# w_out2 in Strassen's form for the first super-block too, and the factors made at 1.4 pieces a step

## The chip, the cores and the metric

One core of a Trainium2 chip runs the whole kernel. The metric is the device time of one execution, in microseconds (us). The engines named below are PE (TensorE, the matmuls), PEld (its weight loads), ACT (ScalarE), DVE (VectorE), POOL (GpSimd) and SP (SyncE, which issues most DMAs).

## What is computed

Three layers follow one another on 2304 tokens of width 512, all in float32.

```python
# retention: 4 batches, 8 heads, 576 positions, 64 wide; Dmat[i, j] = gamma**(i - j) for i >= j
ret = (q @ k.T) * scale * Dmat
x = (ret @ v)                                   # 2304 x 512
h = x @ w_in                                    # 512 -> 2048
g = where(h >= 1, h, where(h <= -1, 0, (h + 1)**2 / 4))
x = g @ w_out                                   # 2048 -> 512
out = ((x @ w_a) * (x @ w_b)) @ w_out2          # 512 -> 1536 -> 512
```

The change concerns the last line alone. Float32 precision is reached by splitting each operand into a rounded upper part and the rest, so that one product takes three matmuls (upper by upper, rest by upper, upper by rest; `HL`, line 479).

## The kernel before

Work is written as a program over tiles of 128 partitions. A planner puts it into one queue per engine when the program is built (`schedule_with_timeline_sim`, line 1380): an instruction that was written earlier goes first, but one that waits for data or for a free buffer is passed by later ones. So plain matmuls of one piece of work stand in the gaps of another. The first part, down to line 1193, is ordered by hand.

Stage 0 is the retention with the first w_in pieces. Stages 1 and 2 (the loop at line 1211) take the other pieces of w_in and w_out, one `step` for each pair of a piece and a block of 384 or 512 tokens: `l1` makes 12 matmuls, `act1` the activation on ACT and DVE, `l2` of the step before 12 more. Beside them runs `maker` (line 325), a generator that turns w_a and w_b, and in `last_tiles` (line 359) w_out2, into the seven left factors of Strassen's product, in Winograd's form. Each `yield` ends a piece of it. It converts two raw 64-bit tiles into `stage` (one buffer; ACT lines 200 and 201, DVE lines 207, 210, 217), takes four sums and differences, splits every factor into its two parts (ACT cast, DVE subtraction) and stores them to DRAM (`q`, `o`). There are 60 pieces for w_a and w_b and 30 for w_out2, one pair of w_out2 tiles in five. `make_more` (line 397) makes one piece when two weight tiles are free; in stages 1 and 2 it is called as often as `credit` allows, which grows by PACE x width / 384 a step (line 1229).

Weights live in a pool of 17 tiles of 512 KB, and one more. `take` and `used` count them. `load_to` (line 413) fetches finished factors on SP's queue in the order of `loads`; it keeps `least` tiles free.

The third layer handles the tokens in three super-blocks of 768 (the loop at line 1285). Each has twelve `Quad`s, one for each of w_a and w_b and six pairs of w_out2's rows; a quad is seven products of six matmuls, into the accumulators named qx, qy and qz, and two quads meet in an elementwise product. In super-blocks 1 and 2 this product goes by `act2_blocks` into four blocks per three pairs, and `second_layer` (line 978) multiplies them with w_out2's factors: seven products over three pieces r, 12 matmuls each (`l2_product`). The right operands come from `cut` (line 927): ACT casts a block into a buffer of the pool `sp`, DVE subtracts the rest; `next_half` orders a cut one turn ahead of its product. `minus` makes the differences of blocks, `keep` (line 832) evacuates an accumulator on ACT.

In super-block 0 it is otherwise. `act2` multiplies 384 columns at a time, `split_g` splits, and `l2_2` (line 1030) multiplies with plain w_out2 tiles, which `last_tiles` keeps as `weights[f]`: the first half of the tokens into the accumulators `acc` between the quads (`fill`), the other half afterwards into `late`. So plain w_out2 tiles occupy weight tiles until their last use, and the pool `y` holds results until then.

Of the kernel before, what the change touches and what calls it, by code (L numbers as in the profile page):

```python
# [20 lines left out]
P = 128  # L21
# [13 lines left out]
NF2 = 12  # L35
HT = 384
WBUFS, WBUFS2 = 17, 1
PACE = 1.2
MID = 288
CHUNKS = 4  # L40
YBUFS = 5
# [83 lines left out]
def retention_ffn_kernel(  # L125
# [233 lines left out]
    def last_tiles(f0, f1):  # L359


        o11, o21, o12, o22 = range(4)
        for p in range(f0 // 2, f1 // 2):
            r, i = divmod(p, 2)
            st = stage.tile([P, 8, 256], F32, tag="stage", name="stage")
            for j in range(2):
                f = 2 * p + j
                t = convert(raws2.next(), st[:, 2 * j:2 * j + 2, :].rearrange("p c f -> p (c f)"))
                weights[f] = split(t, take(f))
                raws2.more()  # L370
                yield
            for j, f, m in ((0, 2 * p, 0), (2, 2 * p + 1, 0), (6, 2 * p + 1, 1)):
                nc.sync.dma_start(
                    od[j][r][:, i, :].rearrange("p (a c) -> p a c", a=2),
                    weights[f][:, :, 256 * m:256 * m + 256].bitcast(F32),
                )
            sub, add = nc.vector.tensor_sub, nc.vector.tensor_add
            add(st[:, S1], st[:, o21], st[:, o22])
            sub(st[:, S2], st[:, S1], st[:, o11])
            sub(st[:, S3], st[:, o11], st[:, o21])  # L380
            sub(st[:, S4], st[:, o12], st[:, S2])
            yield
            for k, pair in enumerate((((1, S1), (3, S2)), ((4, S4), (5, S3)))):
                t = take(("mo", p, k)).tile([P, 2, 512], F32R, tag="w", name="qo")
                for n, (j, o) in enumerate(pair):
                    hi, lo = t[:, n, :256], t[:, n, 256:]
                    nc.scalar.copy(hi, st[:, o])
                    nc.vector.tensor_sub(lo, st[:, o], hi.bitcast(F32))
                    nc.sync.dma_start(od[j][r][:, i, :], t[:, n, :].bitcast(F32))
                used(("mo", p, k))  # L390
                yield
            if i == 1:
                banked.update(("o", j, r) for j in range(7))

# [11 lines left out]
    loads = []  # L406
    for n in range(B * S // (2 * HT)):
        loads += [(n, p, k) for p in range(NF2 // 2) for k in range(7)]
        if n:
            loads += [(n, "o", j, r) for j in TURNS for r in range(NF2 // 4)]  # L410
    begun2, held_back = [0], [0]

    def load_to(n):
        while begun2[0] < min(n, len(loads)):
            key = loads[begun2[0]]
            least = 3 if raws2.taken < len(second) else 1 + held_back[0]
            if key[1:] not in banked or free() < least:
                return
            t = weights[key] = take(key).tile([P, 2, 512], F32R, tag="w", name="w2")
            nc.sync.dma_start(t.bitcast(F32), (od[key[2]] if key[1] == "o" else qd[key[1]])[key[-1]])  # L420
            begun2[0] += 1
# [455 lines left out]
            if w == 0:  # L877
                self.c21 = keep(self.x)

    gs2, late = {}, {}  # L880

    def split_g(t):
        g = gpool.tile([P, 2, WIDE], F32R, tag="g", name="g2")
        nc.scalar.copy(g[:, 0, :HT], t)
        nc.vector.tensor_sub(g[:, 1, :HT], t, g[:, 0, :HT].bitcast(F32))
        return g

    def act2(qa, qb):

        n, p, _ = qa.at  # L890
        f = 2 * p
        nc.vector.tensor_mul(qa.c11, qb.c11, qa.c11)
        nc.vector.tensor_mul(qa.c21, qb.x[:, :HT], qa.c21)  # L893
        for j, t in enumerate((qa.c11, qa.c21)):
            gs2[f + j] = t if f + 2 == NF2 else split_g(t)
        for j, (ca, cb) in enumerate(((qa.c12, qb.c12), (qa.c22, qb.c22))):
            t = late[f + j] = (
                ca if f + 2 == NF2
                else ypool[0].tile([P, HT], F32, tag="y", name="gl") if f
                else cpool.tile([P, 512], F32, tag="conv", name="gl")[:, :HT]  # L900
            )
            nc.vector.tensor_mul(t, ca, cb)

    blocks, halves = {}, {}

    def store(n, p, name):
# [120 lines left out]

    spool = [None]

    def l2_2(ys, f, g):  # L1030
        w = weights[f]
        for m in (0, 2, 3, 1):
            ws = slice(m * P, (m + 1) * P)
            for i, (a, z) in enumerate(((0, 0), (1, 0), (0, 1))):
                mm(
                    ys[m][:, :HT], w[:, a, ws], g[:, z, :HT],
                    f == 0 and i == 0, f == NF2 - 1 and i == 2,
                )

    def o_out(ys, t0):  # L1040
        for m, y in enumerate(ys):
            t = t2pool.tile([P, TB], F32, tag="t2", name="ost")[:, :HT]
            (nc.scalar.copy if m % 2 else nc.vector.tensor_copy)(t, y[:, :HT])
            nc.sync.dma_start(out[m * P:(m + 1) * P, t0:t0 + HT], t)


    warm = wpool.tile([P, 2, 512], F32R, tag="w", name="warm")
    nc.vector.memset(warm[:, 0, :].bitcast(F32), 0.0)
    wacc = acc.tile([P, 512], F32, tag="acc0", name="wacc")
# [36 lines left out]
    ))  # L1086
    depth[0] = 4

    stage, ypool, first_sb = None, [None], ExitStack()
    gs = {}  # L1090
    prev = None
    steps, goes_on = [], NWIDE - 1
# [178 lines left out]
        if at_end:  # L1271
            load_to(9)

    ypool[0] = first_sb.enter_context(tc.tile_pool(name="y", bufs=NF2 - 4))
    quad, waiting, pending = None, [], [lambda: l2(prev)]

    def fill(n=1):
        for _ in range(n):
            if pending:
                pending.pop(0)()  # L1280

    def ahead2(n):
        load_to(begun2[0] + n)

    for n in range(NSB):
        early = accs(NCC) if n == 0 else None
        if n:
            held_back[0] = 4
        for p in range(NF2 // 2):
            for w in range(2):  # L1290
                while n == 0 and w and not all(f in weights for f in (2 * p, 2 * p + 1)):
                    next(work)
                while (n, p, 3 + 3 * w) not in weights and (p, 3 + 3 * w) not in banked:
                    next(work)
                ahead2(8)
                q = Quad(n, p, w)
                q.begin()
                if quad:
                    quad.fourth()
                q.second()  # L1300
                late_fill = []
                if quad:
                    quad.fifth()
                    if quad.at[2] == 0:
                        other = quad
                    elif n:
                        act2_blocks(other, quad)
                    else:
                        act2(other, quad)
                        f = 2 * quad.at[1]  # L1310
                        late_fill = [
                            (lambda f=f: l2_2(early, f, gs2.pop(f))) for f in (f, f + 1)
                        ]
                fill(2)
                q.third()
                pending += late_fill
                quad = q
                if n == 0:
                    for _ in range(2):
                        make_more(0)  # L1320
                if (p, w) == (0, 0):
                    load_y(n + 1)
                elif (p, w) == (3, 0):
                    making = right(n + 1)
                if p > 2 and w == 0:
                    make_right()
                ahead2(8)

        if n:
            second_layer(n, quad, other)  # L1330
            quad = None
            continue
        split_of = {f: split_g(late[f]) for f in range(2)}
        fill(1)
        quad.fourth()
        fill(1)
        quad.fifth()
        act2(other, quad)
        assert not pending
        quad = None  # L1340
        for _ in work:
            pass
        ahead2(8)
        ys2 = [bank(f"late{m}") for m in range(NCC)]
        todo = [(ys2, f, late.pop(f)) for f in range(NF2)]
        todo += [(early, f, gs2.pop(f)) for f in (NF2 - 2, NF2 - 1)]
        for j, (acc_of, f, _) in enumerate(todo):
            if j + 2 < len(todo):
                split_of[j + 2] = split_g(todo[j + 2][2])
            l2_2(acc_of, f, split_of.pop(j))  # L1350
            if acc_of is early or f < NF2 - 2:
                used(f)
            make_right()
            ahead2(2)
            if j == NF2 - 1:
                o_out(ys2, first_token(n) + HT)
        o_out(early, first_token(n))
        first_sb.close()
        spool[0] = ctx.enter_context(tc.tile_pool(name="sp", bufs=3))


_W = ["moe_w_in", "moe_w_out", "moe2_w_a", "moe2_w_b", "moe2_w_out"]
# [21 lines left out]
```

## Time and profile before

| | |
|---|---|
| median of 3 runs | 877.51 us (873.87 to 878.70) |
| the profiled execution, its own time | 871.92 us |
| its span, first to last instruction | 870.1 us |
| PE, PEld busy | 860.0 us, 816.5 us |
| DVE, ACT, POOL busy | 573.6 us, 443.4 us, 81.8 us |
| stages 1 and 2 | about 205 to 478 us |
| super-block 0, 1, 2 | about 478 to 607, 607 to 738, 738 to 870 us |

The rows come from one profiled execution. A row of matmuls has the modelled duration of one, which overlaps the next; the rate is read from the time that many of them take together. "Idle before" is the time that an engine stood still ahead of an instruction, with the instruction that released it. Idle time of an engine other than PE costs nothing by itself.

### The profile page before, as it was taken

How to read it: one execution, taken by the hardware profiler on the slowest of the kernel's cores; microseconds unless marked ns; L12 is line 12 of the kernel's file. 1: busy time of each engine (PE TensorE's matmuls, PEld its weight loads, DVE VectorE, ACT ScalarE, POOL GpSimd, SP SyncE). 2: the span in 40 equal slices, each digit the busy share in tenths (PEclk: the TensorE clock that was granted, in tenths of full speed). 3: DMA queues.
4: the chain of work that ended last, by engine and by line, in shares of the span. 5: the costliest groups of instructions: out<-in, count | busy, mean ns of one | idle time of the engine just before them, and what ended most of it. 6: DMA issues, size and time to landing. Idle time of an engine off the chain costs nothing.

```text
span 870.1 us, 15774 instructions
## 1 busy us (share of the span) xinstructions
PE 860.0 (99%) x6068; PEld 816.5 (94%) x6068; DVE 573.6 (66%) x1056; ACT 443.4 (51%) x869; POOL 81.8 (9%) x124
## 2 busy tenths in 40 slices
PE   8899999999999999999999999999999999999998
PEld 5799999999998888888999999999999999999998
DVE  5787566576777888688779858652356675346465
ACT  4555455576656767656666545442334453233252
POOL 2323233110010111010001000000000000000000
PEclk9999999999999999999999999999999999999999
DMA  9996572799778876696599998769547589847583
GB/s 336 369 347 249 195 276 59 272 370 330 246 250 324 291 255 197 218 324 234 178 343 381 394 355 275 255 238 326 178 135 258 175 296 412 307 144 250 184 298 138
DMA packets 82555, 231.98 MB, mean 267 GB/s; under 512 B 7976, under 2 KB 27736, under 8 KB 81712
## 3 DMA queue, kind: packets, MB, share of 16 engines
q1 hardware_dynamic: 72064, 190.58, 61.0%
q0 software_dynamic: 10400, 40.37, 13.3%
q8 instruction: 48, 0.79, 0.4%
q14 instruction: 27, 0.22, 0.1%
q10 hardware_dynamic: 16, 0.02, 0.0%
HBM read 170.65 MB, written 60.29 MB: 265 GB/s over the span
## 4 chain that ended last, share of the span: by engine, by line
PE 96%; DMA 2%; issue 0%; DVE 0%; SPq 0%; ACT 0%
PE acc L162 34%; PE ph L162 23%; PE qx L162 17%; PE qy L162 9%; PE late L162 4%; PE qz L162 4%; PE po L162 3%; DMA uw<-in_qkv 1%; PE s L162 1%; DMA u<-in_qkv 1%; SPq L465 0%; DVE keep L893 0%; DVE keep L859 0%; ACT keep L837 0%; ACT ost L1023 0%
## 5 line engine op out<-in xcount | busy, mean ns | idle before, releaser
L162 PE MATMUL acc<-g,w 128*128 128x384 f32 (+1 forms) x1176 | 244.9, 351 | 0.0
L162 PEld LDWEIGHTS acc<-g,w 128*128 128x128 f32 x1176 | 210.0, 188 | 14.5
L162 PE MATMUL qx<-tx,w 128*128 128x384 f32 x864 | 165.1, 334 | 0.2 <-ACT keep L837 0.2
L162 PEld LDWEIGHTS qx<-tx,w 128*128 128x128 f32 x864 | 151.0, 188 | 0.7 <-ACT keep L837 0.5
L837 ACT COPY keep<-qx 128x384 f32<-128x384 f32 x126 | 59.7, 481 | 136.8 <-PE qx L162 130.4
L162 PE MATMUL ph<-x,w 128*128 128x384 f32 x672 | 128.4, 338 | 0.0
L162 PEld LDWEIGHTS ph<-x,w 128*128 128x128 f32 x672 | 117.9, 189 | 1.1 <-issue 0.2
L162 PE MATMUL ph<-xw,w 128*128 128x512 f32 x360 | 89.0, 389 | 0.0
L162 PE MATMUL qy<-tx,w 128*128 128x384 f32 x432 | 86.6, 334 | 0.0
L691 DVE SCALAR_TENSOR_TENSOR t<-t,ph 128x384 f32<-128x384 f32 (+1 forms) x86 | 51.2, 597 | 53.0 <-ACT t L689 52.5
L688 ACT ACTIVATE t<-ph 128x384 f32<-128x384 f32 (+1 forms) x86 | 45.4, 528 | 73.7 <-PE ph L162 70.0
L162 PEld LDWEIGHTS ph<-xw,w 128*128 128x128 f32 x360 | 67.5, 188 | 13.9
L162 PE MATMUL acc<-sp,w 128*128 128x384 f32 x432 | 77.8, 334 | 0.0
L162 PEld LDWEIGHTS qy<-tx,w 128*128 128x128 f32 x432 | 75.9, 188 | 0.0
L162 PEld LDWEIGHTS acc<-sp,w 128*128 128x128 f32 x432 | 75.1, 188 | 0.0
L696 ACT CAST g<-t 128x384 fp32r<-128x384 f32 (+1 forms) x86 | 47.2, 548 | 39.4 <-DVE t L691 34.2
L698 DVE TENSOR_TENSOR g<-t,g 128x384 fp32r<-128x384 f32 (+1 forms) x86 | 51.7, 603 | 21.1 <-ACT g L696 21.0
L932 DVE TENSOR_TENSOR sp<-gb,sp 128x768 fp32r<-128x768 f32 x42 | 40.1, 956 | 20.5 <-ACT sp L931 20.2
L689 ACT ACTIVATE t<-t 128x384 f32<-128x384 f32 (+1 forms) x86 | 48.4, 563 | 2.3
L931 ACT CAST sp<-gb 128x768 fp32r<-128x768 f32 x42 | 35.0, 837 | 28.4 <-PE acc L162 18.8
L201 ACT ACTIVATE raw<-raw 128x512 int32<-128x512 uint32 x68 | 45.6, 672 | 4.1 <-DMA raw<-in_moe_w_out 4.0
L872 DVE TENSOR_TENSOR keep<-keep 128x384 f32<-128x384 f32 x36 | 20.0, 555 | 36.0 <-ACT keep L837 36.0
(117 smaller groups left out, 1005.0 us busy)
## 6 DMA issues: line engine op xcount, KB each, us to landing
w<-q SPq DMA_DIRECT2D x126, 512.0 KB, 5.8
q<-q SPq DMA_DIRECT2D x42, 512.0 KB, 5.0
w<-o SPq DMA_DIRECT2D x42, 512.0 KB, 4.4
u<-in_qkv SPq DMA_DIRECT2D x32, 512.0 KB, 8.0
raw<-in_moe_w_out POOLq DMA_DIRECT2D x18, 512.0 KB, 6.4
xw<-xdw SPq DMA_DIRECT2D x4, 2048.0 KB, 9.4
raw<-in_moe_w_a POOLq DMA_DIRECT2D x12, 512.0 KB, 5.7
x<-xd SPq DMA_DIRECT2D x4, 1536.0 KB, 9.8
```

The costliest lines, as they stand in the source:

```text
L162: return nc.tensor.matmul(o, l, r, start=start, stop=stop, skip_group_check=goes_on)
L201: nc.scalar.activation(r, low, AF.Copy, scale=2.0 ** -29)
L688: nc.scalar.activation(t, ph[:, :n], AF.Relu, bias=0.5, scale=0.5)
L689: nc.scalar.activation(t, t, AF.Square)
L691: nc.vector.scalar_tensor_tensor(out=t, in0=t, scalar=1.0, in1=ph[:, :n], op0=ALU.min, op1=ALU.max)
L696: hi = nc.scalar.copy(g[:, 0, :], t)
L698: anchor[:] = [hi, nc.vector.tensor_sub(g[:, 1, :], t, g[:, 0, :].bitcast(F32))]
L837: kept_by[0] = nc.scalar.copy(t, o[:, :HT])
L872: nc.vector.tensor_add(self.c22, self.c22, self.s5)
L931: nc.scalar.copy(t[:, 0], b)
L932: nc.vector.tensor_sub(t[:, 1], b, t[:, 0].bitcast(F32))
```

## The change

`last_tiles` makes no plain tiles any more: it converts into `stage` alone and makes all seven factors there by cast and subtraction. `loads` lists w_out2's factors for super-block 0 too. Its elementwise product goes by `act2_blocks`, its second layer by `second_layer`; `act2`, `split_g`, `l2_2`, `o_out`, the pool `y` and the plain matmuls between the quads are gone. `sp` has 2 buffers in super-block 0 (in the place of `y`) and 3 in the others, as before. `held_back` is 4 from the start, and `load_to` keeps two tiles more while raw tiles are left. PACE goes from 1.2 to 1.4.

```diff
-PACE = 1.2
+PACE = 1.4
             for j in range(2):
-                f = 2 * p + j
-                t = convert(raws2.next(), st[:, 2 * j:2 * j + 2, :].rearrange("p c f -> p (c f)"))
-                weights[f] = split(t, take(f))
+                convert(raws2.next(), st[:, 2 * j:2 * j + 2, :].rearrange("p c f -> p (c f)"))
                 raws2.more()
                 yield
-            for j, f, m in ((0, 2 * p, 0), (2, 2 * p + 1, 0), (6, 2 * p + 1, 1)):
-                nc.sync.dma_start(
-                    od[j][r][:, i, :].rearrange("p (a c) -> p a c", a=2),
-                    weights[f][:, :, 256 * m:256 * m + 256].bitcast(F32),
-                )
...
-            for k, pair in enumerate((((1, S1), (3, S2)), ((4, S4), (5, S3)))):
+            turns = (((0, o11), (1, S1)), ((3, S2), (4, S4)), ((5, S3), (2, o12)), ((6, o22),))
+            for k, pair in enumerate(turns):
...
-                yield
+                if k % 2:
+                    yield
...
-        if n:
-            loads += [(n, "o", j, r) for j in TURNS for r in range(NF2 // 4)]
+        loads += [(n, "o", j, r) for j in TURNS for r in range(NF2 // 4)]
...
-            least = 3 if raws2.taken < len(second) else 1 + held_back[0]
+            least = 1 + held_back[0] + 2 * (raws2.taken < len(second))
...
-    ypool[0] = first_sb.enter_context(tc.tile_pool(name="y", bufs=NF2 - 4))
-    quad, waiting, pending = None, [], [lambda: l2(prev)]
+    spool[0] = first_sb.enter_context(tc.tile_pool(name="sp", bufs=2))
+    quad = None
+    l2(prev)
...
-        if n:
-            held_back[0] = 4
+        held_back[0] = 4
...
-                while n == 0 and w and not all(f in weights for f in (2 * p, 2 * p + 1)):
-                    next(work)
...
-                    elif n:
+                    else:
                         act2_blocks(other, quad)
-                    else:
-                        act2(other, quad)
...
-                fill(2)
                 q.third()
...
         for _ in work:
             pass
-        ahead2(8)
-        ys2 = [bank(f"late{m}") for m in range(NCC)]
...
+        second_layer(n, quad, other)
+        quad = None
+        if n == 0:
+            first_sb.close()
+            spool[0] = ctx.enter_context(tc.tile_pool(name="sp", bufs=3))
```

## Rows read from the trace of the kernel before

**Rows 1.** The page, its first part: busy time, share of span, instructions.
```profile
PE 860.0 (99%) x6068; PEld 816.5 (94%) x6068; DVE 573.6 (66%) x1056; ACT 443.4 (51%) x869; POOL 81.8 (9%) x124
```
**Rows 2.** The page, the chain that ended last, share of the span by engine.
```profile
PE 96%; DMA 2%; issue 0%; DVE 0%; SPq 0%; ACT 0%
```
**Rows 3.** Busy time by stretch: stretch, its length, engines in turn, PEclk, DMA share, GB/s.
```profile
core 0: us, PE busy (x) PEld busy (x) DVE busy (x) ACT busy (x) POOL busy (x), PEclk, DMA share, GB/s
...
300.00:354.00 54.00, 54.00 (x240) 44.72 (x239) 45.39 (x87) 37.73 (x73) 8.18 (x12) 1.00 0.66 231
354.00:457.00 103.00, 103.00 (x501) 90.95 (x500) 77.74 (x156) 63.33 (x128) 6.70 (x10) 1.00 0.75 262
457.00:478.00 21.00, 20.93 (x121) 20.61 (x119) 20.30 (x40) 13.37 (x29) 2.61 (x4) 1.00 1.01 380
478.00:520.00 42.00, 41.85 (x241) 41.85 (x242) 29.10 (x61) 22.26 (x49) 2.12 (x4) 1.00 1.03 392
...
607.00:694.00 87.00, 87.00 (x504) 87.00 (x503) 45.19 (x75) 30.76 (x60) 0.00 (x0) 1.00 0.56 189
694.00:738.00 44.00, 44.00 (x255) 44.00 (x255) 29.30 (x37) 19.77 (x30) 0.00 (x0) 1.00 0.93 346
```
**Rows 4.** Groups by shape, 478 to 607 us: count, busy us, mean ns, idle before.
```profile
L162 PE MATMUL acc<-g,w 128*128 128x384 f32 x144 | 28.8, 334 | 0.0
...
L162 PE MATMUL late<-g,w 128*128 128x384 f32 x144 | 25.6, 335 | 0.7 <-DVE keep L893 0.7
```
**Rows 5.** PE in order of time, second layer of super-block 1: start, length, what, count.
```profile
699.36 23.39 PE L162 MATMUL acc<-sp,w 128*128 128x384 f32 x134
722.59 3.63 PE L162 MATMUL late<-sp,w 128*128 128x384 f32 x20
```
**Rows 6.** PE in order of time, the two pauses, with the idle time before.
```profile
478.15 1.34 PE L162 MATMUL qx<-tx,w 128*128 128x384 f32 x6 [0.21 <-ACT keep L837]
...
579.46 20.57 PE L162 MATMUL late<-g,w 128*128 128x384 f32 x117 [0.65 <-DVE keep L893]
```
**Rows 7.** ACT in order of time, second layer of super-block 1.
```profile
714.47 0.84 ACT L931 CAST sp<-gb 128x768 fp32r<-128x768 f32 x1 [1.24 <-PE acc L162]
716.55 0.84 ACT L931 CAST sp<-gb 128x768 fp32r<-128x768 f32 x1 [1.24 <-PE acc L162]
...
722.27 0.48 ACT L837 COPY keep<-acc 128x384 f32<-128x384 f32 x1 [0.72 <-PE acc L162]
```
**Rows 8.** DVE in order of time, the same place.
```profile
715.34 0.96 DVE L932 TENSOR_TENSOR sp<-gb,sp 128x768 fp32r<-128x768 f32 x1 [1.12 <-ACT sp L931]
...
720.49 0.96 DVE L935 TENSOR_TENSOR gb<-gb 128x768 f32<-128x768 f32 x1
```
**Rows 9.** Groups by shape, whole span: DVE's work for maker and quads.
```profile
L210 DVE SCALAR_TENSOR_TENSOR stage<-raw,stage 128x512 uint32<-128x512 uint32 x36 | 24.5, 687 | 0.7
L217 DVE CUSTOM_DVE_ANT_0 stage<-raw,stage 128x1024 uint16<-128x1024 uint16 x36 | 24.4, 686 | 1.3
...
L859 DVE TENSOR_TENSOR keep<-qz,keep 128x384 f32<-128x384 f32 x36 | 20.0, 556 | 33.3 <-PE qz L162 28.7 <-ACT keep L837 4.4
...
L207 DVE TENSOR_SCALAR stage<-stage 128x512 uint32<-128x512 uint32 x36 | 15.0, 421 | 3.4 <-ACT stage L200 3.3
...
L388 DVE TENSOR_TENSOR qo<-stage,qo 128x256 fp32r<-128x256 f32 x24 | 9.3, 419 | 4.8 <-ACT qo L387 4.8
...
L229 DVE TENSOR_TENSOR w<-stage,w 128x512 fp32r<-128x512 f32 x12 | 8.1, 684 | 0.1
```
**Rows 10.** SP's queue in order of time: the maker's last stores.
```profile
566.06 0.80 SPq L389 DMA_DIRECT2D o<-qo  x2
```
**Rows 11.** DMA issues: tile, count, KB each, median us to landing.
```profile
w<-q SPq DMA_DIRECT2D x126, 512.0 KB, 5.8
...
w<-o SPq DMA_DIRECT2D x42, 512.0 KB, 4.4
...
o<-qo SPq DMA_DIRECT2D x24, 256.0 KB, 5.4
```

More of the change, by code (lines that the diff above doesn't have):

```diff
@@ L878, in fifth @@
                 self.c21 = keep(self.x)
[L880 to L902, printed above, removed]
     blocks, halves = {}, {}
@@ L1028, in retention_ffn_kernel @@
     spool = [None]
[L1030 to L1044, printed above, removed]
     warm = wpool.tile([P, 2, 512], F32R, tag="w", name="warm")
@@ L1087, in retention_ffn_kernel @@
     depth[0] = 4
-    stage, ypool, first_sb = None, [None], ExitStack()
+    stage, first_sb = None, ExitStack()
     gs = {}
@@ L1272, in retention_ffn_kernel @@
             load_to(9)
-    ypool[0] = first_sb.enter_context(tc.tile_pool(name="y", bufs=NF2 - 4))
-    quad, waiting, pending = None, [], [lambda: l2(prev)]
[L1277 to L1280, printed above, removed]
+    spool[0] = first_sb.enter_context(tc.tile_pool(name="sp", bufs=2))
+    quad = None
+    l2(prev)
     def ahead2(n):
@@ L1285, in retention_ffn_kernel @@
     for n in range(NSB):
-        early = accs(NCC) if n == 0 else None
-        if n:
-            held_back[0] = 4
+        held_back[0] = 4
         for p in range(NF2 // 2):
             for w in range(2):
-                while n == 0 and w and not all(f in weights for f in (2 * p, 2 * p + 1)):
-                    next(work)
                 while (n, p, 3 + 3 * w) not in weights and (p, 3 + 3 * w) not in banked:
@@ L1300, in retention_ffn_kernel @@
                 q.second()
-                late_fill = []
                 if quad:
@@ L1305, in retention_ffn_kernel @@
                         other = quad
-                    elif n:
+                    else:
                         act2_blocks(other, quad)
-                    else:
-                        act2(other, quad)
[L1310 to L1313, printed above, removed]
-                fill(2)
                 q.third()
-                pending += late_fill
                 quad = q
@@ L1327, in retention_ffn_kernel @@
                 ahead2(8)
[L1329 to L1340, printed above, removed]
         for _ in work:
             pass
-        ahead2(8)
-        ys2 = [bank(f"late{m}") for m in range(NCC)]
[L1345 to L1359, printed above, removed]
+        second_layer(n, quad, other)
[3 more added lines that the diff above has]
+            spool[0] = ctx.enter_context(tc.tile_pool(name="sp", bufs=3))
 _W = ["moe_w_in", "moe_w_out", "moe2_w_a", "moe2_w_b", "moe2_w_out"]
```

## The prediction

> **What bounds the kernel now.** I read the page's engine totals first, then the chain that ended last, then busy time by stage. TensorE (PE) is busy 860.0 of 870.1 us [rows 1], and the chain runs through it for 96% of the span [rows 2]. Of the missing 10 us the stages listed hold 0.2 [rows 3] and one pause 0.65 [rows 6]; the rest lies before 300 or after 738 us. By stage it is the same: from 300 to 457 us and again from 607 to 738 us PE has no idle time at all, while DVE, the next engine, stands between 52% and 84% [rows 3]. One stretch is different: from 457 to 478 us DVE is busy 20.30 of 21 us and the DMA engines are at their top (share 1.01, then 1.03 at 392 GB/s) [rows 3]; PE is still busy there, because plain matmuls of older work fill its waits. So this kernel's time is a count of matmuls, plus whatever waits the planner's order cannot fill. PE's granted clock is 1.00 throughout [rows 3], so no stage has speed to gain.
>
> What is one matmul worth? Not its listed duration: rows of 334 ns overlap. In super-block 1's second layer 134 of them take 722.59 - 699.36 = 23.23 us [rows 5], so one of 384 columns costs 23.23/134 = 173.4 ns. A stretch of super-block 1 agrees: 504 in 87.00 us, 172.6 ns [rows 3].
>
> **Part 1, the product itself.** Super-block 0's plain second layer is 12 tiles x 4 output chunks x 3 matmuls x 2 halves = 288; the rows show 144 into acc and 144 into late [rows 4]. Strassen's form is 7 products x 3 tiles x 2 chunks x 2 outputs x 3 = 252. 36 fewer, all on PE, which is the bound: 36 x 173.4 ns = -6.24 us. This term has one answer, since the two later super-blocks already run the same 252. The Trainium skill (TensorE: Matmul & The Clock Gate, Back-to-back issue gap) gives an isolated gap of N/2.4 + 2.5 ns, 162.5 ns for 384 columns; this case's 173.4 ns is 7% more. By the page the term would be -5.85 us, an estimate; the measurement decides.
>
> **Part 2, a pause that goes.** After 572 us PE waits once, 0.65 us, for a DVE add ahead of a late matmul [rows 6]. That code (act2, split_g, l2_2) is gone. What is late next at this place is a half of a block being cut, which is part 3. -0.65 us. The other pause, 0.21 us at 478 us [rows 6], stays.
>
> **Part 3, two buffers for halves instead of three.** In super-blocks 1 and 2 the pool sp has 3 buffers; in super-block 0 the change gives it 2, since stage still takes space. The trace shows what that means. A cut is an ACT cast of 0.84 us and a DVE subtraction of 0.96 us that begins 0.03 us after it [rows 7, 8]. The casts start 2.08 us apart, each released by a PE product [rows 7]: with three buffers a cut already waits for a buffer, but has two products (4.16 us) until its turn. With two it has one, 12 x 0.1734 = 2.08 us. Counted from the last matmul's issue slot (the last product in acc ends at 722.59, the ones before it every 2.08 us back, at 716.35 and 714.27 among others; casts begin 0.2 us after these [rows 5, 7]): 0.20 + 0.84 + 0.03 + 0.96 = 2.03 us, plus about 0.05 us to PE. It is needed at 2.08 us for the first matmul's upper part, which the cast alone writes, and at 2.25 us for the lower part. Alone it fits, with 0.05 to 0.2 us to spare. What can come ahead of it on its two engines: 8 evacuations at 0.48 us on ACT (3.8), 6 block differences at 0.96 us on DVE (5.8) and 6 adds at 0.55 us (3.3), 12.9 us per second layer [rows 7 to 9]. Between cuts ACT is free 1.24 us and DVE 1.12 us [rows 7, 8], so each fits a gap once; they hurt where two fall together: at the turns where x is evacuated while blocks are subtracted, and at the last block, whose cut needs the buffer of a product that has only just ended. I count two such places at about 0.5 us each. Cost: nothing to 12.9 us, I take 1.0, near the low end, because the casts' spacing row shows the gaps empty in most products.
>
> No fill hides it: the next super-block's first weights come after 21 loads of w_out2 factors in the load list and need free tiles.
>
> **Part 4, the maker and its pace.** PACE is a credit per step in stages 1 and 2. These have 25 steps of 384 and 30 of 512 tokens: 25 x 1.2 + 30 x 1.6 = 78 turns before, 25 x 1.4 + 30 x 1.867 = 91 after. Following take and used through the code, at these turns the free tiles never fall below two, so the maker stands at 67 of its 90 pieces before and at 80 after when super-block 0 begins. Two turns a quad (42 matmuls, 7.28 us) then do the rest: before in the twelfth quad, which the trace confirms by its last o<-qo store at 566.06 [rows 10]; after in the fifth, about 40 us ahead of the second layer. Nothing waits for a factor.
>
> A pair of w_out2 pieces costs about the same in either form. DVE: two conversions at 0.421 + 0.687 + 0.686 us, then 4 + 7 operations at 0.42 us, 8.2 us; before, 4 + 4 and two splits at 0.684 us, 8.3 us [rows 9]. Stores are 7 of 256 KB either way. So only place changes: 13 pieces x 8.2/5 = 21 us of DVE move ahead into 205 to 478 us. In 300 to 354 us the count gives two more pieces, 3.3 us on 45.39 of 54: 90%, not full [rows 3]. Cover is the one-step distance between act1 and its l2. Cost 0 to 3 us, taken 0.2.
>
> **Part 5, the quads without plain matmuls between.** In super-blocks 1 and 2 quads alone leave PE no gap [rows 3]. In super-block 0 the first five also meet the maker. DVE in their 36.4 us: two pairs 16.4, 15 adds at 0.556 us 8.3, eight block products at 0.55 us 4.4, one cut and two differences 2.9, together 32.0: 88%, following 97% [rows 3, 8, 9]. DMA: 17.5 weight tiles, about 4 raw tiles of the same 512 KB and 14 stores of 256 KB [rows 11], 15 MB or 410 GB/s against 392 seen, short by 0.7 MB, a tile and a half; the nine tiles that load_to(9) fetched before are the cover, and without it this would be 2 us. 21 more loads of factors (11 MB) come later, as in 694 to 738 us, where 346 GB/s left PE no idle time [rows 3]. Behind the raised tile reserve on SP's queue (held_back now 4, 7 while making) stand only loads that super-blocks 1 and 2 issue under the same 5. Cost 0 to 3 us, taken 0.5.
>
> **Sum.** -6.24 - 0.65 + 1.0 + 0.2 + 0.5 = -5.2 us. On the profiled execution 871.92 becomes 866.7 (span 864.9); the runs' median is 877.51, 5.6 above that execution, and it becomes 872.3.
>
> **Rivals.**
> First, two buffers cost more than the product saves (the other side). If the evacuations, differences and adds stand ahead of the cuts, every product waits a little; it decides at 6.9/19 = 0.36 us for each product after the first two, one evacuation's worth. At its full price, -6.9 + 12.9 = +6.0: 883.5 on the median; half of it, no change, 877. For it: a margin of 0.05 us. Against: idle 1.24 us ahead of most casts. The Trainium skill (Perfetto Trace Analysis, Optimization Strategy) says that the same gap repeating on the engine that should be full can mean too few buffers for the next tile; with three buffers no run here shows such gaps. 0.08 for slower, 0.10 for no change.
> Second, the start of super-block 0 stalls: DVE goes over 100%, or the weights come late: 3 us, and with part 3's 1.0 the gain is 2.9: 874.6. For it: DVE 97% and DMA 1.03 at this place. Against: ten pieces left there instead of 23. 0.15.
> Third, the pace: stages 1 and 2 lose 3 us: the gain is 2.4: 875.1. 0.05.
> Fourth, it does not do what it says. If tiles run out, make_more's turns pass unused, factors come as late as before (566 us), and a store's 5.4 us and a load's 4.4 us [rows 11] come between them and a product due near 560 us: 16 us, 887. The count speaks against it. 0.02.
>
> **Chances.** Forecast 0.60, the rest as given. About 4.4 us, 0.5%, is what a measurement can tell from no change. In the forecast's own case some tenth stays under it: faster 0.55, same 0.35, slower 0.10. Range: from the full gain of 6.9 with runs 2.4 under the median (the spread shown) to a loss of 1.5: 868.2 to 879.0.
>
> **What would show it.** After: 36 fewer matmuls; no late<-g, acc<-sp products in three stretches; PE idle between about 550 and 600 us is part 3 itself (under 2 us right, over 6 wrong), with releaser DVE sp or ACT sp. The last o<-qo store near 520 us shows the pace; PE idle from 457 to 500 us would show the second rival; idle before 457 the third. DMA waits ahead of acc<-sp would make me wrong on the loads.

## The result and the profile after

The changed kernel takes 881.18 us (median; 877.08 to 884.09), the kernel before 873.68 us in the same rounds: a ratio of 1.0078, 95% interval 1.0060 to 1.0095. Forecast was a gain of 5.2 us; there is a loss of 7.5 us. (The 877.51 us that the forecast of 872.3 started from was the median of three runs; over these sixteen the same kernel stands at 873.68.) The profiled execution took 882.12 us, its span is 880.4.

The page of the kernel after: its engine totals and the shares of the chain that ended last.

```profile
PE 863.8 (98%) x6032; PEld 816.6 (93%) x6032; DVE 589.1 (67%) x1074; ACT 448.5 (51%) x877; POOL 82.4 (9%) x124
...
PE 91%; DMA 5%; DVE 2%; ACT 1%; issue 1%; SPq 0%; ACTq 0%
```

The 36 matmuls are gone, 6032 against 6068 [rows 1]. But DMA holds 5% of the chain where it held 2%, and PE 91% where it held 96% [rows 2]. The next view says where: busy time by stretch (columns as in [rows 3]), kernel after.

```profile
354.00:457.00 103.00, 102.33 (x489) 89.17 (x487) 79.19 (x168) 62.92 (x133) 8.31 (x13) 1.00 0.80 288
457.00:478.00 21.00, 20.79 (x119) 20.23 (x118) 21.00 (x38) 16.62 (x35) 2.80 (x4) 1.00 0.79 280
478.00:520.00 42.00, 36.13 (x193) 35.49 (x193) 30.26 (x66) 18.98 (x43) 0.57 (x2) 0.92 1.02 388
470.00:480.00 10.00, 10.00 (x58) 9.77 (x57) 10.00 (x21) 7.81 (x18) 2.04 (x3) 1.00 0.53 163
480.00:490.00 10.00, 4.49 (x25) 3.85 (x23) 7.72 (x18) 2.90 (x8) 0.55 (x1) 0.95 1.02 382
490.00:500.00 10.00, 9.64 (x41) 9.64 (x42) 3.35 (x7) 4.57 (x11) 0.00 (x0) 0.71 1.03 414
```

Two of these stretches of ten in the kernel before.

```profile
470.00:480.00 10.00, 9.79 (x56) 9.47 (x55) 9.26 (x22) 5.22 (x13) 1.02 (x2) 1.00 1.01 388
480.00:490.00 10.00, 10.00 (x60) 10.00 (x59) 8.79 (x19) 5.88 (x13) 1.06 (x2) 1.00 1.05 380
```

From 354 to 457 us PE loses only 0.67 us. Behind that two things stand out. PE loses 5.87 of 42 us in 478 to 520, where it lost 0.15 before [rows 3]. And in 470 to 480, DVE has no idle time at all while the DMA engines move 163 GB/s instead of 388: a hole between stretches in which their share is 1.02 or more.

PE in order of time, kernel after: the lines with idle time from 455 to 625 us, and the one behind the longest.

```profile
456.66 0.99 PE L162 MATMUL acc<-g,w 128*128 128x384 f32 x4 [0.67 <-ACT g L690]
469.17 1.30 PE L162 MATMUL qz<-tx,w 128*128 128x384 f32 x6 [0.21 <-PE qy L162]
484.22 1.32 PE L162 MATMUL qx<-tx,w 128*128 128x384 f32 x6 [1.04 <-DVE keep L853]
490.36 2.29 PE L162 MATMUL qx<-tx,w 128*128 128x384 f32 x6 [4.82 <-ACT keep L831]
492.45 3.75 PE L162 MATMUL qy<-tx,w 128*128 128x384 f32 x12
```

The pause of 4.82 us costs more than its length: the six matmuls behind it take 492.45 - 490.36 = 2.09 us, 0.35 us each where 0.173 is usual. PE's clock, granted at 2.4 GHz ahead of the pause, fell to its lower level of 1.2 GHz inside it, at 488.9 us, and rose again at 495.7 us (a mean of 0.71 in 490 to 500).

For each matmul of 384 or 512 columns from 28 us on, take by how much the next one starts later than 173.4 ns (228 for 512 columns) after it. The sum is 6.63 us in the kernel before, 19.34 after. Of the 12.7 us difference, about 10 lie between 456 and 496 us (called the seam from here: stage 2's last block and super-block 0's first quads), 7.5 of them the pause at 490 and its slow matmuls; 2.3 us lie in super-block 0's second layer and just behind it. -6.24 + 12.7 is 6.5 us, near the 6.2 us by which the last matmul is later once both traces are laid together at their first FFN matmul (the first into ph). That one is itself 4.3 us later in this execution, at 35.5 us. Start-up runs the same code in both kernels, and in the thirteen profiles below this matmul begins between 31.2 and 34.2 us, so those 4.3 us belong to the execution and not to the change.

What ends the pause? The chain of work that ended last, between 478 and 491 us, kernel after (start, length, what).

```profile
478.48 0.55 DVE keep L860
479.03 0.33 DVE qo L382
479.37 1.33 DVE yin L746 x3
480.70 0.20 issue
480.90 8.91 DMA yf<-yin
489.81 0.02 issue
489.83 0.49 ACT keep L831
490.32 0.04 issue
490.36 1.65 PE qx L162 x4
```

The quad's evacuation (keep, ScalarE's copy out of an accumulator) takes its tile from the pool t2. Its seven tiles are shared with the four yin tiles in which stage 2's last block is summed, and a yin tile comes free only when its store into yf has landed: the evacuation starts 0.02 us after that. DVE makes the sums at 479 to 481 us. SP issues the first store at 480.90, behind the last of six factor stores, and this store, the one that matters, lands 8.9 us later. The prediction named neither the pool nor this store.

SP's waits from 440 to 492 us (line waited for, us in total, times, longest), kernel after:

```profile
SPq L383 <- DVE qo L382: 15.9, 8, 7.1
SPq L383 <- DVE stage L374: 8.1, 1, 8.1
```

and the longest three in the kernel before, where no store of a w_out2 factor is among them:

```profile
SPq L420 <- DMA q<-q: 6.6, 3, 5.4
SPq L753 <- DVE yin L752: 5.8, 5, 3.6
SPq L753 <- DVE stage L341: 3.9, 1, 3.9
```

SP's queue in order of time, kernel after, three lines of it:

```profile
468.03 0.32 SPq L383 DMA_DIRECT2D o<-qo  x1
...
476.91 3.90 SPq L383 DMA_DIRECT2D o<-qo  x6
480.90 5.02 SPq L747 DMA_DIRECT2D yf<-yin  x4
```

L383 is the store of a w_out2 factor, L747 that of a sum. With the faster pace the maker is at these factors just here; in the kernel before the first such store went out at 473.38 us, behind the first store of a sum (472.49). SP stands 15.9 + 8.1 = 24 us in front of the factor stores until DVE, full with the maker, with the quads' right operands (right()) and with act1, has made the factors. Behind them in SP's order stand the weight loads and the stores of the sums. That is the hole.

### The profile page after: what moved, and what is told of

Same layout as the page of the kernel before. It is cut to its first block, busy times and chain, and to the rows that moved or that the text cites. A ratio compares the mean times of both kernels' runs of the same rounds, so it can differ in the third digit from the quotient of the medians.

```text
span 880.4 us, 15817 instructions
## 1 busy us (share of the span) xinstructions
PE 863.8 (98%) x6032; PEld 816.6 (93%) x6032; DVE 589.1 (67%) x1074; ACT 448.5 (51%) x877; POOL 82.4 (9%) x124
## 4 chain that ended last, share of the span: by engine, by line
PE 91%; DMA 5%; DVE 2%; ACT 1%; issue 1%; SPq 0%; ACTq 0%
PE acc L162 32%; PE ph L162 22%; PE qx L162 16%; PE qy L162 8%; PE qz L162 4%; PE po L162 4%; PE s L162 2%; PE late L162 2%; DMA w<-q 2%; DMA w<-o 1%; DMA yf<-yin 1%; DMA o<-qo 1%; PE idle L162 1%; DVE tx L778 0%; PE wacc L162 0%
## 5 line engine op out<-in xcount | busy, mean ns | idle before, releaser
L162 PE MATMUL acc<-g,w 128*128 128x384 f32 (+1 forms) x1032 | 215.6, 355 | 0.7 <-ACT g L690 0.7
L162 PEld LDWEIGHTS acc<-g,w 128*128 128x128 f32 x1032 | 184.7, 188 | 15.5 <-ACT g L690 1.0
L162 PE MATMUL acc<-sp,w 128*128 128x384 f32 x648 | 116.7, 335 | 0.7 <-ACT sp L901 0.6
L162 PEld LDWEIGHTS acc<-sp,w 128*128 128x128 f32 x648 | 112.5, 188 | 1.5 <-ACT sp L901 0.9
L902 DVE TENSOR_TENSOR sp<-gb,sp 128x768 fp32r<-128x768 f32 x63 | 60.2, 956 | 33.7 <-ACT sp L901 33.5
L901 ACT CAST sp<-gb 128x768 fp32r<-128x768 f32 x63 | 52.6, 837 | 49.6 <-PE acc L162 34.2
```

The source lines that it names most:

```text
L162: return nc.tensor.matmul(o, l, r, start=start, stop=stop, skip_group_check=goes_on)
L901: nc.scalar.copy(t[:, 0], b)
L902: nc.vector.tensor_sub(t[:, 1], b, t[:, 0].bitcast(F32))
```

## Experiments

There are four theories. A: the pace itself, by crowding ScalarE and VectorE at the seam. B: the shared t2 tiles, with the plain matmuls no longer there to cover a late one. C: the head of SP's queue, that is, factor stores which wait for VectorE while loads and stores behind them could go. D: VectorE is simply full, and the sums are late whatever the queue does. Differences below are against the kernel before in the same rounds (873.4 to 874.0 us).

**Undo the pace: e1.**
```diff
-PACE = 1.4
+PACE = 1.2
```


> The changed kernel with the old pace of 1.2 pieces a step (80 of 91 turns become about 69 done when super-block 0 begins, the rest inside it). Kernel before 873.7 us, changed 881.2 us. Theory A (pace): the extra maker turns ahead of the seam 456 to 496 us crowd ScalarE, VectorE and the DMA queues, so that the last partial sums leave late; with the old pace the 5.0 us wait of the quad's evacuation and the 18 matmuls at half clock behind it go: 871 to 874 us. Theory B (buffers and lost cover): the wait comes from the four partial-sum tiles that share a pool with the quads' evacuations and from the plain matmuls that no longer stand in the first quads; neither depends on the pace: the gap near 490 us stays at 4 us or more and the time at 879 to 883 us. If the maker's rest inside super-block 0 delays factors, up to 4 us more in either case, seen as waits of the second layer on w loads.


Measured 882.97 us, ratio 1.010 (1.0078 to 1.0121), +9.0 us. PE's two large pauses in it:

```profile
481.98 1.84 PE L162 MATMUL qx<-tx,w 128*128 128x384 f32 x6 [2.73 <-ACT keep L831]
...
570.10 20.19 PE L162 MATMUL acc<-sp,w 128*128 128x384 f32 x101 [3.88 <-DMA w<-o]
```

The seam's pause shrinks to 2.73 us (and is again followed by matmuls at half clock), and no store ends it: here the evacuation stands on ScalarE behind the maker's conversion.

```profile
479.24 1.22 ACT stage L200 x2
480.45 1.11 ACT raw L201 x2
481.56 0.37 ACT keep L831
```

The last factors are now stored from 560.58 us on, and the second layer waits for their reload (3.88 us). Theory A's time is refuted, and B's pause of 4 us too. By the count used above e1 loses 4.7 us at the seam, where the changed kernel loses 10.6, but 14.5 behind it, where that one loses 3.8. So the pace does make the seam dearer, and the old pace is still no way out: the changed kernel needs the factors earlier than the old one did.

**The pace alone: e2**, the kernel before with PACE = 1.4.


> The kernel before with the new pace of 1.4 and nothing else. Before 873.7 us. Theory A (pace): the wait at the seam appears here too, and the time is 879 to 883 us. Theory B (lost cover): twelve plain matmuls of 174 ns still stand at the seam and 12 more after each second quad, a late buffer is covered up to 2 us and the time stays at 873 to 876 us. A pace that costs in stages 1 and 2 would show as later starts of the matmuls ahead of 440 us by more than 1 us net of start-up; expected none.


Measured 881.38 us, 1.0084 (1.0062 to 1.0106), +7.4 us. Theory B fell here as it was put: the plain matmuls still stand at the seam and do not save it. The pauses:

```profile
478.83 1.32 PE L162 MATMUL qx<-tx,w 128*128 128x384 f32 x6 [0.57 <-ACT keep L837]
481.58 1.31 PE L162 MATMUL qx<-tx,w 128*128 128x384 f32 x6 [1.43 <-ACT keep L837]
489.12 1.80 PE L162 MATMUL qx<-tx,w 128*128 128x384 f32 x6 [3.10 <-DMA w<-q]
```

The longest is a weight load: SP stood 7.5 and 4.3 us in front of the w_out2 stores there, and the DMA engines moved 199 GB/s in 460 to 470 us, against 380 in 457 to 478 before [rows 3]. It looks like the same wait with another victim; e11 tests that.

**The sums in tiles of their own: e3.** The changed kernel, pace 1.4, with the last block's four yin tiles in two weight tiles.
```diff
 def fetch_y(i, b):
     for m in range(NCC):
+        if (i, b) == (2, PASSES[2][-1]):
+            if m % 2 == 0:
+                two = take(("y", m)).tile([P, 2, 512], F32R, tag="w", name="yt").bitcast(F32)
+            t = yin[b, m] = two[:, m % 2, :TB]
+        else:
             own, tag, n = (ywide[0], "yw", WIDE) if b > 1 else (t2pool, "t2", TB)
...
             (nc.gpsimd if stage is None else nc.sync).dma_start(to[:, m, :], t)
+            if (i, b) == (2, PASSES[2][-1]) and m % 2:
+                used(("y", m - 1))
```


> The changed kernel, but the four partial-sum tiles of stage 2's last block lie in two weight tiles, not in the pool of seven that the quads' evacuations write. Theory B (buffers): the evacuation at 485 to 490 us no longer waits for their stores to land; the 4.8 us pause and the 2.7 us at half clock behind it go, 881.2 - 7.5 = 873 to 875 us. Theory A (pace crowds the engines): the evacuation then waits behind the maker's casts on ScalarE or VectorE instead and no more than 3 us comes back: 878 to 881 us. Two weight tiles less for loads ahead: a wait of PE on w loads of up to 2 us would show that the tiles are missed.


Measured 869.57 us, 0.9949 (0.9931 to 0.9967): 4.4 us faster than the kernel before, some 11.9 less than the change as it is. SP stands in front of the factor stores nearly as long (13.7 + 6.0 us), VectorE is full from 450 to 480 us (10.00 of 10 in each ten), and the sums' stores go out late and take 6.7 to 9.4 us to land, but PE does not wait for them. The stores, and PE's longest pause at the seam:

```profile
475.07 4.98 SPq L752 DMA_DIRECT2D yf<-yt  x4
...
487.80 1.28 PE L162 MATMUL qx<-tx,w 128*128 128x384 f32 x6 [0.16 <-DMA w<-q]
```

For the changed kernel theory B holds: the path from the late stores to PE runs through the shared tiles, and the half clock goes with the pause. VectorE alone (theory D) does not stop PE there: with DVE as full, e3 loses 1.0 us at the seam by the count, the changed kernel 10.6. The time is below B's 873 to 875 us; e3's trace shows 9.5 of the 11.9 us, and where the rest comes from is open.

**The tiles apart in the kernel before: e12** (the edit of e3 alone, pace 1.2).


> The kernel before (873.7 to 874.0 us) with nothing but the last block's partial sums apart from the quads' evacuations: the cell that says whether the third experiment's 11.6 us belong to the changed kernel alone. In the kernel before no evacuation waits for a store's landing (its one pause at the seam is 0.2 us), so theory B gives 873 to 875 us; 870 us or less would mean that the tiles held the kernel before back too, and that the change itself brings little. Two weight tiles less for loads ahead could cost up to 2 us.


Measured 872.47 us, 0.998 (0.9967 to 0.9992), -0.9 us. Sharing the tiles cost the kernel before almost nothing, so e3's gain is the change's own obstacle removed. Against e12, e3 is 3.5 us faster.

**The tiles apart, with the old pace: e5** (e3 with PACE = 1.2).


> The third experiment (partial sums of the last block apart from the quads' evacuations, 869.6 us) with the old pace of 1.2. The first experiment lost 4.7 us at the seam and then 10 us at 538 to 578, where factors of w_out2 were not made when the second layer came. Theory B (buffers own the seam): the seam stays free, only the late factors cost, 869.6 + 8 to 10 = 877 to 880 us. If the new pace is not needed once the seam is free (the late factors were a follow-on of the seam's delay): 869 to 871 us.


Measured 881.96 us, 1.0089 (1.0075 to 1.0103): 12.5 us more than e3, where 8 to 10 were expected. The pauses are now late: 2.62 us at 522 on an evacuation, 1.13 at 530, and 3.09 at 569 for w_out2 factors whose last stores left from 560.79 us on. Behind the seam e5 loses 17.8 us by the count, e3 3.9. So with the tiles apart the new pace is needed.

**The tiles apart in the kernel before, with the new pace: e8.**


> The kernel before with pace 1.4 (second experiment, 881.4 us), the last block's partial sums apart as in the third. Theory B (the shared tiles are how the pace costs): the seam's pauses in it (0.6 + 1.4 us of the quads' evacuations, 3.1 us of a w load, 2 us at half clock) go, 874 to 876 us. If the pace costs through the SP queue (w loads behind the maker's stores and the partial sums' stores) and not through the tiles: the pause of 3.1 us for the w load stays, 878 to 881 us.


Measured 883.19 us, 1.011 (1.0089 to 1.0131): no better than e2, and above both ranges expected. PE waits for weight loads instead:

```profile
471.15 1.33 PE L162 MATMUL qy<-tx,w 128*128 128x384 f32 x6 [0.86 <-DMA w<-q]
...
483.17 1.34 PE L162 MATMUL qx<-tx,w 128*128 128x384 f32 x6 [1.26 <-DMA w<-q]
...
488.88 2.67 PE L162 MATMUL qx<-tx,w 128*128 128x384 f32 x12 [3.33 <-DMA w<-q]
```

Theory B does not explain the pace's cost in that kernel. The queue is the next suspect.

**The factor stores on another queue: e9** (changed kernel), e11 (kernel before with pace 1.4, where the stores of the plain tiles' halves move too), e10 (e3).
```diff
-                    nc.sync.dma_start(od[j][r][:, i, :], t[:, n, :].bitcast(F32))
+                    nc.gpsimd.dma_start(od[j][r][:, i, :], t[:, n, :].bitcast(F32))
```


> The changed kernel with the stores of the w_out2 factors issued by GpSimd, not SyncE; the partial sums stay in the shared pool. In the changed kernel SyncE waited 24 us in 440 to 492 in front of such stores for VectorE, and the DMA engines moved 163 GB/s in 470 to 480 us and some 400 around it. Theory C (head of the SP queue): the hole closes (over 300 GB/s), the last partial sums are stored within 1.5 us of their sums and land before the evacuation needs the tile; its wait of 4.8 us falls under 1.5 us and the half clock behind it goes: 873 to 877 us. Theory D (VectorE is full at the seam and the sums themselves are late; the queue only follows): the wait stays over 3 us: 879 to 883 us. GpSimd's own queue then waits for VectorE, and w_out2's next tiles and the b<-yf loads behind it come later, up to 3 us more.


Measured 876.25 us, 1.0033 (1.0018 to 1.0047): +2.25, so 5.2 of the 7.5 us are back, in theory C's range. In e9 most of the hole closes, and of the pause half is left:

```profile
470.00:480.00 10.00, 9.19 (x53) 8.87 (x52) 10.00 (x24) 5.52 (x13) 4.73 (x8) 1.00 0.95 341
...
483.91 2.29 PE L162 MATMUL qx<-tx,w 128*128 128x384 f32 x6 [2.33 <-ACT keep L831]
```

The pause was to fall under 1.5 us and did not: the evacuation now stands on ScalarE behind a factor's cast, which waits for DVE (full in 460 to 480 us); that much of A and D is true. There is also a new pause of 2.34 us at 453 us, just ahead of the seam, on a cast of ScalarE.


> The kernel before with pace 1.4 (881.4 us) with the stores of the w_out2 tiles and factors issued by GpSimd. With the partial sums apart (883.2 us) three waits of PE for w loads of 0.9 + 1.3 + 3.3 us stayed; SyncE stood 7.5 and 4.3 us in front of such stores there. Theory C: these loads are issued when their tiles come free, the DMA hole at 460 to 470 us (199 GB/s) closes, 874 to 877 us. Theory D or DMA throughput alone: 879 to 883 us.


Measured 878.35 us, 1.0051 (1.0037 to 1.0065): 3.0 us back of 7.4, between the two theories. PE's wait for a w load falls from 3.10 to 2.43 us; SP now stands up to 17.1 us in front of the sums' stores, 26.2 us in all. So the queue's head is a part of the pace's price there; as SP still stood, in front of other stores, this run does not show how large a part, and the remainder I have not separated.


> The third experiment (869.6 us) with the stores of the w_out2 factors issued by GpSimd. With the partial sums apart nothing of PE waits at the seam but 0.7 us in all (w loads, keeps), so theory C gives 868.5 to 870 us; if GpSimd's waits delay the maker or b<-yf, 871 to 874 us.


Measured 872.66 us, 0.999 (0.998 to 0.9999): 3.1 us worse than e3. GpSimd now stands 11.8 us in front of these stores for DVE. A raw tile of w_out2 that it loads at 479.25 us takes 11.84 us to land (6.34 in e3), its conversion falls on DVE at 495.7 to 499 us, and PE pauses 2.73 us at 502 us for a DVE add behind it. In these two kernels moving the stores helped where PE's path stood behind them (e9), and cost where it did not (e10).

**Fewer turns at the seam: e6.** The changed kernel with no maker turn in stage 2's last block.
```diff
         credit += 1.0 if i == 0 else PACE * width(i, b) / TB
+        if (i, b) == (2, PASSES[2][-1]):
+            credit = 0.0
```


> The changed kernel with no maker turn in the last block of stage 2 (five steps, about seven turns moved into super-block 0); the partial sums stay in the shared pool. If the maker's work on VectorE, ScalarE and the SP queue is what makes the last partial sums leave late, they are added and stored 3 to 6 us sooner against the quads, the wait of 4.8 us for their tiles shrinks under 1.5 us, and 4 to 7 us come back: 874 to 877 us. If the stores are late for another reason (the loads of the seam, the b<-yf transfers), the wait stays at 4 us or more: 880 to 883 us. The seven turns moved can make the second layer wait for factors, up to 3 us.


Measured 881.35 us, 1.0082 (1.0061 to 1.0102): no gain, and the pause is 9.67 us. SP's queue in e6 in order of time, and the chain's piece:

```profile
466.33 4.15 SPq L383 DMA_DIRECT2D o<-qo  x7
470.58 4.08 SPq L414 DMA_DIRECT2D w<-q  x6
474.71 3.41 SPq L747 DMA_DIRECT2D yf<-yin  x4
...
474.71 14.94 DMA yf<-yin
```

This miss taught most. The sums are stored six us earlier than in the changed kernel, yet the first of them lands at the same place, 489.65 us. In the 4 us ahead of it six loads of weights (3.1 MB) went out on SP's queue, and from GpSimd two loads of b<-yf (1.6 MB) and two raw tiles (1.0 MB); of the seven factor stores the five whose landing the trace has were down by then. From 474.71 to 489.65 us the DMA engines moved 394 GB/s, 5.9 MB: about what these loads hold. So it isn't enough that the sums are early. Here the loads issued ahead, on either queue, decide when a store lands, and the tile is held until then. The expectation's other branch, the loads of the seam, holds.

**Order of the plain matmuls: e4.** The changed kernel with the last twelve plain matmuls behind the first quad's second product, as before.
```diff
-    l2(prev)
+    pending = [lambda: l2(prev)]
...
+                if pending:
+                    pending.pop()()
                 q.third()
```


> The changed kernel, but the last twelve plain matmuls of stage 2's second layer are issued behind the first quad's second and third product, as in the kernel before, and not ahead of the first quad. If the lost order is the cause (they covered the first wait, and now nothing does): 2 to 3 us back, 878 to 879.5 us. Theory B (buffers): the last partial sums are then added 3 quarter-products later, their stores land about 2 us later, and what the twelve matmuls cover is lost again: 880 to 883 us. Theory A (pace): no change, 881 us.


Measured 881.05 us, 1.0077 (1.0060 to 1.0095): the same. Its pause is 6.69 us, ended by the evacuation, which waited for a yf store of 9.78 us. The order shows no effect on the time.

**The price of two buffers: e7** (e3 with two buffers of halves in super-blocks 1 and 2 too).
```diff
-            spool[0] = ctx.enter_context(tc.tile_pool(name="sp", bufs=3))
+            spool[0] = ctx.enter_context(tc.tile_pool(name="sp", bufs=2))
```


> The third experiment (869.6 us) with two buffers of cut halves, not three, in the second and third super-blocks too. It prices the prediction's term for two buffers, +1.0 us a super-block taken and 12.9 at most. By the third experiment's own pauses in super-block 0 (0.7 us of ACT sp and 0.15 beside it): 870.5 to 872 us. If two buffers cost nothing by themselves, 869.6 to 870 us; if the pauses of super-block 0 were cut short by its loads, 875 us or more.


Measured 872.90 us, 0.9994 (0.9978 to 1.0010): 3.4 us more than e3 for two super-blocks, 1.7 each, 0.9 above the upper end expected. The same two places appear in super-block 0 of e3 and in super-block 1 of e7; here a cut in e7, and the evacuation at the end of e3's super-block 0:

```profile
700.50 21.16 PE L162 MATMUL acc<-sp,w 128*128 128x384 f32 x118 [0.61 <-ACT sp L908]
```

```profile
606.02 1.31 PE L162 MATMUL qx<-tx,w 128*128 128x384 f32 x6 [0.95 <-ACT keep L838]
```

**Both last copies on VectorE: e13** (e3, with the output copy that stood on ScalarE moved).
```diff
-                        (nc.scalar.copy if c else nc.vector.tensor_copy)(t, b[:, :HT])
+                        nc.vector.tensor_copy(t, b[:, :HT])
```


> The third experiment (869.6 us) with both of a super-block's last evacuations on VectorE, where ScalarE had one of the two. With two buffers of halves ScalarE's 0.48 us copy stands ahead of the next quad's evacuation, and PE loses 1.1 us at 604 us; the two-buffer experiment showed the same 1.1 us in the second super-block. If that is half of the price of two buffers: 868 to 869 us, and the pause at 604 under 0.6 us. If the evacuation is bound by the matmuls ahead of it and not by ScalarE: 869.3 to 870.3 us.


Measured 867.62 us, 0.9943 (0.9922 to 0.9963), the fastest of all. e3's pause at 606 us is gone from the trace: ScalarE's copy ahead of the next quad's evacuation was its cause. (A new one of 0.86 us stands at 487 us, on a DVE add.) The ratio can't be told from e3's (0.9931 to 0.9967), so the time of this edit by itself is open; against the kernel before the gain is 5.75 us.

## Why the prediction was wrong, point by point

**Part 1** was right in count (36 fewer), and its price fits: with the seam free, e3's trace loses 3.2 us more between matmuls than that of before (9.84 and 6.63), so -6.24 + 3.2 = -3.0 us, beside a measured -4.4 with an interval of about 1.6 to each side. **Part 2** was right: no late<-g and no DVE add in that place.

**Part 3** was right in kind and low in size: 1.0 taken, 1.7 by e7. One of the two places was named rightly (a cut, released by ScalarE); the other, ScalarE's output copy ahead of the next super-block's first evacuation, was not seen. The first rival (12.9 us) is refuted: its 0.36 us for every product appears nowhere.

**Part 4 failed, with the step "only place changes" and its cost of 0 to 3 us, taken 0.2.** The place was even right (the last seven factor stores go out from 513.38 to 518 us, near the 520 forecast), and stages 1 and 2 lose next to nothing: from 168 to 412 us the matmuls of both kernels keep one distance (4.57 to 4.62 us, but for a few that the planner put in another order), which refutes the third rival. But the moved pieces bring their stores with them, and I weighed these as bytes, not as instructions of an in-order queue that wait for VectorE. I asked what the pace does where VectorE has room (300 to 354 us) and not where it arrives: at the seam, where DVE stood at 20.30 of 21 us [rows 3]. In the kernel before this pace alone costs 7.4 us (e2). In the changed kernel the same pace costs little once nothing on PE's path hangs on the late stores (e3: 1.0 us at the seam).

**Part 5 failed likewise, with "cost 0 to 3 us, taken 0.5".** Parts 4 and 5 together took 0.7 us for what is about 10 at the seam. Its sums were near (388 GB/s at a share of 1.02 in 478 to 520, against 410 forecast), but a sum says whether a stretch fits, not who stands behind whom in it. Two questions were missing: what the quad's evacuation writes into, and who holds that tile until when. The nine tiles of load_to(9), named as the cover, covered the weights; nothing covered the t2 tiles. In the kernel before the last block's stores took 9.5 to 10.0 us to land (three of four; the trace lacks the first's landing), no less than after (6.4 to 9.3), and no evacuation waited for them; that the plain matmuls between the quads gave them this time is argued and not shown by a run. The second rival named the place and the sign (PE idle from 457 to 500), with 3 us for what is 10, since it counted neither a store's landing nor the clock behind a pause.

The Trainium skill (DMA: Bandwidth & Descriptors, Anatomy of one DMA — SWDGE (gpsimd) path) states that a DMA's wait on a semaphore happens on the issuing sequencer, ahead of dispatch. The trace agrees: SP's 24 us. The Trainium skill's same page (section Issuing engines are not separate DMA queues) says that starting DMAs from several engines saves only the time to start them. In e9 more than that went with the issues: SP no longer stands 24 us in front of these stores, and 5.2 us of the kernel's time came back; how much of this the issues alone would give no run shows.

What stays open: why the kernel before loses 4.35 us at pace 1.4 even with its stores on GpSimd (e11), and how much of what is left at the seam in e9 is VectorE. No run took work off VectorE there.

## To carry to other kernels

When a change moves work, list what it issues on each in-order queue at the place where it arrives, and what stands behind it there; where VectorE is at 97% beside DMA at its top, what you move in comes late, and the question is who waits for it. For each tile that PE's path writes, ask which other use of the pool holds it, and count a store's hold to its landing under load (9 to 15 us at the seam here, 3.4 for the same store elsewhere). And a change that loses may lose to one neighbour: four sums put into two other tiles turned +7.5 us into -4.4.

## What the runs showed of the hardware

The same 192 KB store took 3.4 to 9.3 us to land in the changed kernel, and up to 14.9 in e6, with 5.7 MB of loads issued in the 4 us ahead of it. The row of 5.02 us for four stores at 480.90 is not the price of issuing them: one issue takes 0.32 to 0.73 us, and the last begins 2.5 us after the one before it has ended.

A pause's length alone did not decide on PE's clock. It fell to the lower level at pauses of 2.33 us (e9, at 484 us) and 2.73 us (e1, at 482), and stayed at the full one through 2.34 us in the same e9 (at 453 us), 2.73 us in e10 and even 3.33 us in e8 (1.00 in 490 to 500 us). PE had been busy without a pause for over 40 us ahead of e10's and of e1's; in e9 it had paused 1.07 us shortly before, in e8 1.26 us. What tells these cases apart these runs do not show.
